# Transposes on TensorE as half transposes side by side, in an attention and mixture kernel

## The chip, the cores and the metric

The kernel runs on one core of one Trainium2 chip. The core has TensorE (PE, with its weight loader PEld), VectorE (DVE), ScalarE (ACT), GpSimd (POOL) and SyncE (SP), which issues most DMAs. Matmuls write PSUM, eight banks of 512 fp32 columns; only PE, DVE and ACT reach it. The metric is the device time of one execution in microseconds, less is better.

## The reference

Inputs are q, k, v of 8 batches, 8 heads, 576 positions and 64 features, and weights of four experts. It computes causal attention in a window of 128 positions with a bias by distance, then a mixture of two out of four experts, each of which is again causal attention over all 576 positions:

```python
scores = where(0 <= rel < 128, q @ k.T / 8 - slope * rel, -1e9)
x = softmax(scores) @ v                      # 8 heads -> 512 features
w = softmax over the two largest of x @ w_gate (0 for the others)
for e in range(4):
    a = softmax(causal((x @ wq[e]) @ (x @ wk[e]).T / 8))
    out += w[e] * (a @ (x @ wv[e])) @ wo[e]
```

## The kernel before

**Windowed attention** goes by head pairs g = 0 to 31, two heads of a batch in one. For each, `attn_s` makes scores in PSUM, DVE adds the bias and takes the row minimum, ACT takes the exponential into a tile w with the row sums, `normalise` scales it (POOL or ACT). `attn_t` turns the nine blocks of 128 by 128 on PE, by a matmul with the identity `idt`, four blocks to a bank: two of them are copied to the tile pa (`evac`, on ACT or DVE), the others are multiplied by a mask in `split`, on DVE alone. `attn_pv` multiplies them by v. The first four pairs go through `half_s`, `half_t` and `half_pv`, in two halves of the positions.

**The mixture** follows batch by batch: `qkproj` and `vproj` (PE, 128 by 128 tiles, the rows `wx,WH`, `wx,WL` and `WH,wx`), `gates`, and for each of two expert pairs pr the scores `moe_s` (tile KKm, 64 by 128 tiles, one expert to each half of the rows) and `moe_s_tail` for the last 64 positions (tile MPL), then `moe_norm`, `moe_t`, `moe_pv`, and `moe_wo` for the output. `moe_t` turns, for a column block c, the blocks of rows i >= c, up to four to a bank, and copies each bank with one `evac`; `moe_t_tail` turns the last rows. The 688 transposes are of 128 by 128 elements.

**The order of everything** is a table. The functions only record operations; some record two alternatives, one for each engine that may do it (`nc.any`, as in `evac`). `plan` reads the table ORDER, which names for each place in the program the operation and its alternative; `_pairs` keeps two matmuls together where the second uses the upper 64 rows. `place` then gives buffers in that order, from pools of equal slots (`_Slots`): all PSUM tiles share eight banks `ps`, SBUF tiles share the pools wx, w5, w10 and w2. Since each recorded operation is emitted at one line, nearly all instructions carry the line L1206; the names of tiles tell them apart. In the names of the profile w is any SBUF slot, ps any bank.

Of the kernel before, what the change touches and what calls it, by code (L numbers as in the profile page):

```python
# [20 lines left out]
DM = H * D  # L21
E = 4
# [20 lines left out]
    "s*f1W`V1-2(vs^s?h-4-=jHwAEiW+H8T*Huw8dV60NC$RQLKSIiPF{ilqD)NJ-R!g};b4CLd*A*7b+;Rpu(-sy+J?NsG~-R>Y7E8&Dqv0t1OV&?!lg-1"
    "rV`PZoS77FwTGzPo(j;84rs@HST_?2HL!Tg+LW3Z<#N!Nf<`l5O%K5Z5?e4NCq&i+S-@&qgN$r|9LR-|ZBO6iOw34HXE4-7PL6fnHWW6e*_{z2slu*A#"
    "5r8bMe9!vHeE`B5(7ah?T>dBn{o;X?Tw{P1w9FaEsiCH#bC(=$g|>yA{wKZ0~{*_kVMR#zk=XE(P~o9+P?&80QnYYQEEtRR&uyItx*p?cH$5kt+4>xm="
    ">pnI9ebEVxzRH!R%K!K=m4|?-f^U%U?>jgaqXkhnZ>%75Bn?<p2DDrKs7VIv;;DKBdm`W#faEvkx>-OQ<`=p$zg#Qdu5DFgvx7x-yfWQye-sIt?rycEn"
    "aH&V=ldtA>J2P}cI&qp~lLj|?Y69A1JL#R#`^b1*uHf*ydu_=J}4mcIDx8+#GPvV|+=LKqvIoSG!}e$_^jauREb1~O)c__Rwfv)orgJD?1x;xW$`t<na"
# [1246 lines left out]
```

## Time and profile before

| | us |
|---|---|
| median of 3 runs (497.78 to 498.13) | 497.96 |
| profiled execution, first to last instruction (its span) | 495.4 |
| PE busy | 487.4 |
| DVE busy | 421.3 |
| ACT busy | 359.3 |
| POOL busy | 222.5 |

The profiled execution is known by its span; the median stands 2.6 us above it. PE's records overlap, as each matmul's duration holds its latency: how long PE needs for one is read from the distance of two starts. A row `ps<-idt,w 128*128 128x128` is a transpose: the loaded tile of 128 rows by 128 columns is w, the moving operand idt has 128 columns. An fp32 matmul that is no transpose stands as two records.

### The profile page before, as it was taken

The numbers are of one execution on the slowest core, as the hardware profiler recorded it, in microseconds if no ns is written. First come the engines' busy times: TensorE is split into PE (matmuls) and PEld (weight loads), VectorE is DVE, ScalarE is ACT, GpSimd is POOL, SyncE is SP. The second block draws the span as 40 slices with busy tenths as digits, with TensorE's granted clock in tenths as the row PEclk, the third lists the DMA queues.
The fourth block names the chain that finished last, engine by engine and source line by source line (L and its number), as shares of the span: only waits on it lengthen the run. The fifth ranks groups of instructions, "written<-read, shape, count | busy, mean of one in ns | idle before, by whom it ended". The sixth has DMA issues, their size and how long they took to land.

```text
span 495.4 us, 16247 instructions
## 1 busy us (share of the span) xinstructions
PE 487.4 (98%) x5772; PEld 430.7 (87%) x5772; DVE 421.3 (85%) x1918; ACT 359.3 (73%) x1349; POOL 222.5 (45%) x440
## 2 busy tenths in 40 slices
PE   7999999999999999999999999999999999999996
PEld 5889988997989889898897988989789897899775
DVE  5999998889997897979989799897999869946763
ACT  4968979878958497585976969587694948543951
POOL 3815575252915246071460815625094533453350
PEclk9999999999999999999999999999999999999999
DMA  7979440027122350234240612623152301200033
GB/s 199 294 183 218 114 116 2 7 45 173 51 74 76 107 140 20 58 94 102 83 131 2 178 32 55 193 81 70 61 150 77 103 2 32 84 1 1 2 107 107
DMA packets 29856, 44.91 MB, mean 91 GB/s; under 512 B 9424, under 2 KB 15824, under 8 KB 29776
## 3 DMA queue, kind: packets, MB, share of 16 engines
q1 hardware_dynamic: 29040, 43.42, 32.7%
q8 instruction: 46, 0.75, 0.6%
q10 hardware_dynamic: 736, 0.46, 0.4%
q14 instruction: 34, 0.28, 0.2%
HBM read 34.42 MB, written 9.44 MB: 89 GB/s over the span
## 4 chain that ended last, share of the span: by engine, by line
PE 69%; DVE 1%; issue 0%; ACT 0%
PE ps L1206 69%; DVE w L1206 1%; DVE ps L1206 0%; ACT AHm L1206 0%; DVE ALTm L1206 0%; DVE nm L1206 0%; DVE ALm L1206 0%; DVE mr L1206 0%
## 5 line engine op out<-in xcount | busy, mean ns | idle before, releaser
L1206 ACT COPY w<-ps 128x512 f32<-128x512 f32 (+3 forms) x165 | 78.7, 504 | 49.3 <-PE ps L1206 42.7
L1206 PE MATMUL ps<-wx,WH 128*128 128x288 f32 (+2 forms) x512 | 110.7, 300 | 0.2 <-DVE nm L1206 0.2
L1206 POOL TENSOR_SCALAR w<-w,mr,w 128x512 f32<-128x512 f32 (+3 forms) x128 | 76.4, 609 | 74.5 <-DVE mr L1206 50.8
L1206 ACT ACTIVATE w<-w,nm 128x128 f32<-128x128 f32 x252 | 98.7, 395 | 7.9 <-DVE nm L1206 7.6
L1206 PEld LDWEIGHTS ps<-wx,WH 128*128 128x128 f32 x512 | 83.0, 189 | 2.5 <-DVE ps L1206 0.3
L1206 ACT ACTIVATE w<-w,mnm 128x128 f32<-128x128 f32 (+3 forms) x128 | 70.9, 556 | 14.5 <-DVE mnm L1206 12.7
L1206 PE MATMUL ps<-idt,w 128*128 128x128 f32 x608 | 80.9, 275 | 0.0
L1206 DVE CUSTOM_DVE_ANT_0 w<-ps,tbt 128x128 f32<-128x128 f32 x288 | 72.8, 284 | 5.2 <-PE ps L1206 4.2
L1206 POOL TENSOR_SCALAR w<-w,r 128x128 f32<-128x128 f32 x151 | 54.7, 373 | 49.0 <-DVE r L1206 37.0
L1206 DVE TENSOR_TENSOR w<-ps,tmt 128x256 f32<-128x256 f32 (+2 forms) x96 | 71.2, 771 | 2.8 <-PE ps L1206 2.4
L1206 PEld LDWEIGHTS ps<-idt,w 128*128 128x128 f32 x608 | 68.9, 140 | 3.9 <-issue 1.1
L1206 PE MATMUL ps<-wx,WL 128*128 128x288 f32 (+2 forms) x256 | 70.8, 296 | 0.0
L1206 PE MATMUL ps<-w 64*64 64x192 f32 (+3 forms) x1256 | 59.8, 306 | 2.1 <-DVE ps L1206 1.3
L1206 PE MATMUL ps<-WH,wx 128*128 128x260 f32 x288 | 61.6, 286 | 0.0
L1206 PE MATMUL ps<-w,vt 64*64 64x192 f32 (+4 forms) x1344 | 57.2, 284 | 0.5 <-DMA vt<-in_vd 0.5
L1206 DVE COPY w<-ps 128x512 f32<-128x512 f32 (+3 forms) x85 | 47.5, 565 | 9.2 <-PE ps L1206 8.6
L1206 PEld LDWEIGHTS ps<-w,vt 64*64 64x64 f32 (+1 forms) x1344 | 48.9, 133 | 6.7 <-issue 1.0
L1206 PEld LDWEIGHTS ps<-w 64*64 64x64 f32 (+1 forms) x1256 | 44.4, 134 | 9.1 <-DMA w<-in_hd 2.3
L1206 ACT ACTIVATE w<-w,r 128x128 f32<-128x128 f32 x137 | 48.4, 396 | 5.1 <-DVE r L1206 4.9
L1206 DVE COPY_PREDICATED ps<-mkt,ps 128x256 f32<-128x256 int32 (+2 forms) x160 | 50.5, 329 | 1.4 <-PE ps L1206 0.4
L1206 DVE CUSTOM_DVE_ANT_0 w<-ps,mtt 128x384 f32<-128x384 f32 (+2 forms) x96 | 50.0, 550 | 0.9 <-PE ps L1206 0.7
L1206 PE MATMUL ps<-w,w 128*64 128x64 f32 (+4 forms) x576 | 48.2, 319 | 0.1
(110 smaller groups left out, 978.2 us busy)
## 6 DMA issues: line engine op xcount, KB each, us to landing
w<-in_hd SPq DMA_DIRECT2D x56, 288.0 KB, 4.5
vt<-in_vd SPq DMA_DIRECT2D x28, 320.0 KB, 4.0
out<-w SPq DMA_DIRECT2D x31, 256.0 KB, 3.8
w<-in_hd SPq DMA_DIRECT2D x14, 128.0 KB, 3.8
w<-in_hd SPq DMA_DIRECT2D x56, 32.0 KB, 3.6
w<-in_wall SPq DMA_DIRECT2D x4, 386.0 KB, 5.4
out<-w SPq DMA_DIRECT2D x8, 128.0 KB, 2.7
vt<-in_vd SPq DMA_DIRECT2D x4, 192.0 KB, 6.3
```

What stands on the lines that cost most here:

```text
L1206: getattr(getattr(tc.nc, e), m)(*a, **k)
```

## The change

608 transposes of 128 rows become 1216 of 64 rows by 128 columns. `turn` takes up to eight blocks and two banks; rows 0 to 63 of each block go to the first bank, rows 64 to 127 to the second, in 64 columns for each block, so a pair of instructions uses the two row halves of PE. Each bank is emptied apart, into every second group of 64 columns of the target. `attn_t` turns eight blocks in one call, with two copies of 128 columns and two masks of 768; `moe_t` has four calls for each expert pair, of 8, 8, 4 and 4 blocks, and the last block whole. The 80 that stay whole are those of `half_t` (32), `half_t_tail` (4), the ninth block of `attn_t` (28) and the last block of `moe_t` (16). `_pairs` now holds the two halves together. The SBUF pool w10 has three slots instead of four, w2 six instead of ten, and pools w4 and w1 are new. The table ORDER is another one throughout.

```diff
--- before.py
+++ after.py
@@ -36,85 +36,81 @@
 
 
 ORDER = (
-    "c-obC0azr*b>?)}>#p9N*3L*X5@XF+j20wDfdm}Jh8Sc>zy}t{@C6dc!6&%D9oQfb7Mwr^8@wRF24ryHyf~~44#;5bN~{Go*bu=9EO0=9c=-%5_#lA`Y"
...
+    "c-p;re_Ui)b!WYIPrZBT_onO3)N`uVst5|PP?!M&89G7)1%+&pfd~m~U_!az!e_vMf&qnT$bf>vPNQ_}j`Ro$hTcFzo9<co1Pmy>(_~=-3LnA14j33|2NG"
...
@@ -194,7 +190,7 @@
     two = {}
     for i in range(1, len(ops)):
         e, m, a, k = ops[i]
-        if e != "tensor" or m != "matmul":
+        if e != "tensor":
             continue
         if any(x.ap[0][1] == D and x.offset // x.ap[0][0] >= D for x in a[:2]):
             assert ops[i - 1][0] == "tensor"
@@ -257,8 +253,10 @@
     ps_s = ps_t = ps_a = _Slots(psum, 8, 512, "ps", PSUM)
     xp = _Slots(cp, 5, 2 * S + TAIL, "wx")
     pp = big5 = _Slots(cp, 8, 2 * S + 3 * D, "w5")
-    tp = big10 = _Slots(cp, 4, 2 * (S + TAIL + S), "w10")
-    big2 = _Slots(cp, 10, DM, "w2")
+    tp = big10 = _Slots(cp, 3, 2 * (S + TAIL + S), "w10")
+    tw = _Slots(cp, 4, 2 * DM, "w4")
+    tr = _Slots(cp, 3, P, "w1")
+    big2 = _Slots(cp, 6, DM, "w2")
 
     busy = {"act": 0.0, "dve": 0.0}
 
@@ -560,38 +558,37 @@
 
     ptT = {}
 
-    def split(dst, src, n):
+    def split(dst, src, n, f=0):
         k = src.shape[1]
-        w = tmt[:, :, :n].unsqueeze(1).broadcast_to((P, k, 2, n))
+        w = tmt[:, :, f : f + n].unsqueeze(1).broadcast_to((P, k, 2, n))
         nc.vector.tensor_tensor(dst, src.unsqueeze(2).broadcast_to((P, k, 2, n)), w, mul)
         busy["dve"] += 65 + 1.04 * 2 * k * n
 
+    def turn(name, blocks):
+        ts = [ps_t.tile([P, 8, D], F32, tag="t", name=f"{name}{x}") for x in "lh"]
+        for k, src in enumerate(blocks):
+            for h in range(2):
+                d = slice(D * h, D * h + D)
+                nc.tensor.transpose(ts[h][:, k, :], src[d], idt[d, d])
+        return ts
+
     def attn_t(g, u):
         pt = state[g][2]
-        t = ps_t.tile([P, 4, P], F32, tag="t", name=f"t{g}_{u}")
         if u == 0:
-            ptT[g] = tp.tile([P, PTW], F32, tag="pa", name=f"pa{g}")
-        w = ptT[g]
-        if u < 2:
-            for k in range(4):
-                nc.tensor.transpose(t[:, k, :], pt[:, 5 * (k % 2) + 2 * u + k // 2, :], idt)
-            i = 2 * u
-            if u == 0:
-                evac(w[:, : 4 * P].rearrange("p (h n) -> p h n", h=2)[:, :, :P], t[:, 0:2, :], 2 * P)
-                split(diag_pair(w, 1, 1, P), t[:, 2:4, :], P)
-            else:
-                
-                for k in range(2) if K["sh"] else (None,):
-                    if k is None:
-                        split(diag_pair(w, 2, 2, P), t, P)
-                    else:
-                        split(diag_pair(w, 2 + k, 1, P), t[:, 2 * k : 2 * k + 2, :], P)
+            w = ptT[g] = tp.tile([P, PTW], F32, tag="pa", name=f"pa{g}")
+            ts = turn(f"t{g}", [pt[:, 5 * (k % 2) + 2 * j + k // 2, :] for j in range(2) for k in range(4)])
+            for h in range(2):
+                c = slice(D * h, D * h + D)
+                evac(w[:, : 4 * P].rearrange("p (h n) -> p h n", h=2)[:, :, c], ts[h][:, 0:2, :], P)
+                split(diag_pair(w, 1, 3, D, D * h), ts[h][:, 2:, :], D, D * h)
         else:
+            w = ptT[g]
+            t = ps_t.tile([P, 4, P], F32, tag="t", name=f"t{g}_{u}")
             nc.tensor.transpose(t[:, 0, :], pt[:, 4, :], idt)
             split(diag_pair(w, NQ, 1, TAIL), t[:, 0, :].rearrange("p (h n) -> p h n", h=2), TAIL)
 
-    def diag_pair(w, i, m, n):
-        a = w[:, 4 * P * (i - 1) + P :]
+    def diag_pair(w, i, m, n, f=0):
+        a = w[:, 4 * P * (i - 1) + P + f :]
         return _View(bass.AP(tensor=a.view.tensor, offset=a.offset, ap=[a.ap[0], [2 * P, 2 * m], [3 * P, 2], [1, n]]), a.tensor)
 
     xT = {}
@@ -837,22 +834,24 @@
             scl2(st["p"][pr, "tail"][:, :S], r[:, 0:1], r[:, 1:2])
         busy["dve"] += 300
 
-    def moe_t(b, pr, c, js):
+    def moe_t(b, pr, u):
         st = m2s[b]
-        t = ps_t.tile([P, 512], F32, tag="t", name=f"mt{b}_{pr}_{js[0]}_{c}")
-        pc = big2.tile([P, 512], F32, tag="pt", name=f"mpt{b}_{pr}_{js[0]}_{c}")
-        n = 512 - P * c
-        for k, j in enumerate(js):
-            for i in range(c, NQ):
-                o = n * k + P * (i - c)
-                nc.tensor.transpose(t[:, o : o + P], st["p"][pr, j, i][:, P * c : P * (c + 1)], idt)
-            st["pt"][pr, j, c] = pc[:, n * k : n * k + n]
-        m = n * len(js)
-        if c == NQ - 1:
-            nc.tensor.transpose(t[:, m : m + P], st["p"][pr, "tail"][:, NQ * P :], idt)
-            st["pt"][pr, "tail"] = pc[:, m : m + P]
-            m += P
-        evac(pc[:, :m], t[:, :m], m)
+        parts = ([(0, 0), (1, 0)], [(0, 1), (0, 3), (1, 1), (1, 3)], [(0, 2), (1, 2)], [("tail", c) for c in range(NQ)])[u]
+        n = 8 if u < 2 else 4
+        pc = (tw if u < 2 else big2).tile([P, n * P], F32, tag="pt", name=f"mpt{b}_{pr}_{u}")
+        blocks = []
+        for j, c in parts:
+            i = [c] if j == "tail" else range(c, NQ)
+            st["pt"][pr, j, c] = pc[:, P * len(blocks) : P * (len(blocks) + len(i))]
+            blocks += [(st["p"][pr, j] if j == "tail" else st["p"][pr, j, k])[:, P * c : P * (c + 1)] for k in i]
+        ts = turn(f"mt{b}_{pr}_{u}", blocks)
+        for h in range(2):
+            evac(pc.rearrange("p (a n) -> p a n", n=P)[:, :, D * h : D * h + D], ts[h][:, :n, :], n * D)
+        if u == 3:
+            t = ps_t.tile([P, P], F32, tag="t", name=f"mt{b}_{pr}_4")
+            nc.tensor.transpose(t, st["p"][pr, "tail"][:, NQ * P :], idt)
+            pc = st["pt"][pr, "tail", NQ] = tr.tile([P, P], F32, tag="pt", name=f"mpt{b}_{pr}_4")
+            evac(pc, t, P)
 
     def moe_pv(b, pr, c):
         st = m2s[b]
@@ -875,25 +874,15 @@
             act_copy(AH[:, pr, :512], acc, 512)
             dve_sub(AL[:, pr, :512], acc, AH[:, pr, :512].bitcast(F32), 512)
 
-    def moe_t_tail(b, pr):
-        st = m2s[b]
-        pt = st["p"][pr, "tail"]
-        pcl = big2.tile([P, 512], F32, tag="pt", name=f"mptl{b}_{pr}")
-        t = ps_t.tile([P, 512], F32, tag="t", name=f"mtl{b}_{pr}")
-        for c in range(NQ):
-            nc.tensor.transpose(t[:, P * c : P * c + P], pt[:, P * c : P * c + P], idt)
-        evac(pcl, t, 512)
-        st["ptl"] = pcl
-
     def moe_pv_tail(b, pr):
         st = m2s[b]
-        pcl, pcl2 = st["ptl"], st["pt"][pr, "tail"]
+        pt = st["pt"]
         V2 = st["v2"]
         acc = ps_t.tile([P, 512], F32, tag="t", name=f"mal{b}_{pr}")
         for c in range(NQ + 1):
             for j in range(2):
                 e = 2 * pr + j
-                src = pcl[:, P * c + D * j : P * c + D * j + D] if c < NQ else pcl2[:, D * j : D * j + D]
+                src = pt[pr, "tail", c][:, D * j : D * j + D]
                 nc.tensor.matmul(
                     acc[D * j : D * j + D, :TAIL], V2[:, c, D * e : D * e + D], src,
                     start=(c == 0), stop=(c == NQ),
@@ -1015,11 +1004,11 @@
             else:
                 for c in range(NQ):
                     moe_pv(b, pr, c)
-            live[0] -= 2 if tail else 5
+            live[0] -= 0 if tail else 7
         pend.append((f, 0, b))
 
     def room(n):
-        while live[0] + n > K["tp"]:
+        while live[0] + n > K["tp"] and pend:
             flush()
         live[0] += n
 
@@ -1038,9 +1027,9 @@
             return u
 
         def t_units(g):
-            tt = [(w, lambda c=c: attn_t(g, c)) for c, w in enumerate((0.44, 0.44, 0.12))]
+            tt = [(w, lambda c=c: attn_t(g, c)) for c, w in enumerate((0.88, 0.12))]
             pv = [(2.1, lambda: run(g))]
-            orders = ("tttp",)
+            orders = ("ttp",)
             return tag(g, [(tt if ch == "t" else pv).pop(0) for ch in orders[K["apv"]]])
 
         marks = []
@@ -1084,12 +1073,8 @@
         return us
 
     def t_units(b, pr):
-        us = []
-        for c in range(NQ):
-            for js in ((0,), (1,)) if c < 2 else ((0, 1),):
-                us.append((0.11 * (4 - c) * len(js), lambda c=c, js=js: (room(1), moe_t(b, pr, c, js))))
+        us = [(0.7, lambda u=u: (room((2, 2, 1, 2)[u]), moe_t(b, pr, u))) for u in range(4)]
         us.append((K["pw"], lambda: part(b, pr, 0)))
-        us.append((0.55, lambda: (room(1), moe_t_tail(b, pr))))
         us.append((K["pw"], lambda: part(b, pr, 1)))
         return us
 
```

On PE, behind a group of projections in the middle of the program, before: the transposes (`idt`) follow one at a time, each into the bank of its block (MPL is the tail's tile).

```order
L1206 MATMUL ps_69<-wx_81,WL 128x288
L1206 MATMUL ps_69<-wx_77,WH 128x288 x2
L1206 MATMUL ps_74<-wx_77,WL 128x288
L1206 MATMUL ps_69<-wx_77,WL 128x288
L1206 MATMUL ps_72<-idt,w_86 128x128
L1206 MATMUL ps_71<-idt,MPL_119 128x128 x2
L1206 MATMUL ps_73<-idt,w_89 128x128
L1206 MATMUL ps_76<-idt,w_85 128x128
```

The same engine and kind of place now: two rows to each block, in two banks, one behind the other.

```order
L1191 MATMUL ps_70<-wx_80,WL 128x288
L1191 MATMUL ps_70<-wx_77,WH 128x288 x2
L1191 MATMUL ps_70<-wx_77,WL 128x288
L1191 MATMUL ps_72<-wx_77,WL 128x288
L1191 MATMUL ps_71<-idt,w_84 128x64
L1191 MATMUL ps_74<-idt,w_84 128x64
L1191 MATMUL ps_75<-idt,MPL_121 128x64
L1191 MATMUL ps_76<-idt,MPL_121 128x64
L1191 MATMUL ps_75<-idt,MPL_121 128x64
L1191 MATMUL ps_76<-idt,MPL_121 128x64
```

Transposes stood in the tile shape of the projections; now they stand in pairs of halves, and the shape changes behind the fourth row, where none changed before.

On DVE, at the attention's masks of one pass (`tmt` is the mask; the row of 448 columns is other work), before: masks of 256, 512 and 1024 columns for the tile w_91, of 1024 and 256 for the next.

```order
L1206 TENSOR_TENSOR w_91<-ps_73,tmt 128x2x2x64
L1206 TENSOR_TENSOR w_91<-ps_74,tmt 128x2x2x128
L1206 TENSOR_TENSOR w_91<-ps_75,tmt 128x4x2x128
L1206 TENSOR_TENSOR w_92<-ps_73,tmt 128x4x2x128
L1206 TENSOR_TENSOR w_96<-w_96,ps_71 128x448
L1206 TENSOR_TENSOR w_92<-ps_69,tmt 128x2x2x64
```

The same stretch now: two masks of 768 columns (6x2x64), one copy of 128 and the mask of 256.

```order
L1191 TENSOR_TENSOR w_90<-ps_75,tmt 128x6x2x64
L1191 COPY w_90<-ps_75 128x2x64
L1191 TENSOR_TENSOR w_90<-ps_69,tmt 128x6x2x64
L1191 TENSOR_TENSOR w_90<-ps_73,tmt 128x2x2x64
L1191 TENSOR_TENSOR w_92<-ps_74,tmt 128x2x2x64
```

The mask over four blocks and that over two have become two over six half blocks, and a copy of the first two half blocks stands between them.

On ACT, copies out of PSUM in the middle of the program, behind the projections' results, before: a bank to a copy, of 384 or 512 columns.

```order
L1206 CAST KKm<-ps_75 128x288
L1206 CAST QHm<-ps_76 128x288
L1206 CAST KKm<-ps_74 128x288
L1206 COPY w_97<-ps_72 128x384
L1206 COPY w_102<-ps_70 128x512
L1206 COPY w_101<-ps_75 128x384
L1206 COPY w_100<-ps_73 128x512
```

The same place now: copies of 8x64, 4x64 and 2x64 columns, one for each half.

```order
L1191 CAST QHm<-ps_70 128x288
L1191 CAST KKm<-ps_72 128x288
L1191 CAST KKm<-ps_69 128x288
L1191 COPY w_102<-ps_76 128x512
L1191 COPY w_100<-ps_74 128x4x64
L1191 COPY w_93<-ps_71 128x8x64
L1191 COPY w_91<-ps_72 128x2x64
L1191 COPY w_94<-ps_69 128x8x64
L1191 CAST QJm<-QLm 64x64
L1191 COPY w_94<-ps_76 128x8x64
```

The copies of 384 columns are gone; those of half blocks go to the same slot two by two (w_94).

## Rows read from the trace of the kernel before

**Rows 1.** Page, part 1: engine, busy us (share of the span) xinstructions

```profile
PE 487.4 (98%) x5772; PEld 430.7 (87%) x5772; DVE 421.3 (85%) x1918; ACT 359.3 (73%) x1349; POOL 222.5 (45%) x440
```

**Rows 2.** Chain of waits in order of time: start us, us, what

```profile
175.89 148.14 PE ps L1206 x1661
...
329.07 162.59 PE ps L1206 x1665
```

**Rows 3.** What PE waited for: us in total, times, longest us; first, last

```profile
PE ps L1206 <- DVE ps L1204: 1.3, 1, 1.3
...
PE ps L1206 <- DVE nm L1206: 0.2, 1, 0.2
```

**Rows 4.** Windows: us, busy of each engine, PEclk, DMA share, GB/s

```profile
25.00:50.00 25.00, 25.00 (x373) 22.02 (x371) 24.22 (x127) 19.50 (x87) 9.53 (x24) 1.00 0.85 199
50.00:75.00 25.00, 25.00 (x353) 23.28 (x350) 24.78 (x121) 21.98 (x92) 16.00 (x33) 1.00 0.43 113
125.00:150.00 25.00, 24.92 (x342) 21.83 (x341) 23.72 (x103) 18.52 (x70) 12.90 (x19) 1.00 0.28 77
225.00:250.00 25.00, 25.00 (x359) 21.53 (x360) 24.05 (x108) 19.05 (x71) 5.89 (x11) 1.00 0.38 92
425.00:450.00 25.00, 25.00 (x282) 23.12 (x281) 16.28 (x59) 11.26 (x38) 10.72 (x17) 1.00 0.01 1
```

**Rows 5.** Windows, the transposes alone (tile idt): PE, PEld

```profile
125.00:150.00 25.00, 5.48 (x43) 4.76 (x43) 1.00 0.28 77
225.00:250.00 25.00, 4.32 (x37) 3.75 (x34) 1.00 0.38 92
```

**Rows 6.** Timeline, PE, 26 transposes: start us, us, what

```profile
284.69 3.00 PE L1206 MATMUL ps<-idt,w 128*128 128x128 f32 x26
```

**Rows 7.** Timeline, PE, transposes, then KKm pairs

```profile
167.60 0.71 PE L1206 MATMUL ps<-idt,w 128*128 128x128 f32 x5
168.24 0.39 PE L1206 MATMUL ps<-KKm,QHm 64*128 64x256 f32 x2
168.46 0.28 PE L1206 MATMUL ps<-KKm,QLm 64*128 64x256 f32 x2
168.58 0.28 PE L1206 MATMUL ps<-KKm,QHm 64*128 64x256 f32 x2
```

**Rows 8.** Groups by form, PE: shapes xcount | busy us, mean ns

```profile
L1206 PE MATMUL ps<-w,vt 64*64 64x192 f32 x672 | 35.2, 327 | 0.5 <-DMA vt<-in_vd 0.5
...
L1206 PE MATMUL ps<-w,vt 64*64 64x64 f32 x448 | 19.3, 220 | 0.0
```

**Rows 9.** Timeline, PE, transposes behind 64 by 64 tiles

```profile
251.17 0.66 PE L1206 MATMUL ps<-idt,w 128*128 128x128 f32 x4
```

**Rows 10.** What the weight loader waited for; longest total first

```profile
PEld ps L1206 <- issue: 21.6, 98, 0.4
```

**Rows 11.** Groups by form, ACT

```profile
L1206 ACT COPY w<-ps 128x384 f32<-128x384 f32 x33 | 15.5, 484 | 3.3 <-PE ps L1206 1.5 <-DVE w L1206 1.5
...
L1206 ACT COPY w<-ps 128x256 f32<-128x256 f32 x42 | 15.4, 369 | 26.4 <-PE ps L1206 23.2 <-DVE w L1206 2.1 <-DVE lg L1206 0.8
...
L1206 ACT COPY xq<-ps 128x64 f32<-128x64 f32 x13 | 2.7, 205 | 3.6 <-PE ps L1206 3.6
```

**Rows 12.** Groups by form, DVE

```profile
L1206 DVE TENSOR_TENSOR w<-ps,tmt 128x1024 f32<-128x1024 f32 x32 | 38.8, 1218 | 1.3 <-PE ps L1206 1.1
...
L1206 DVE TENSOR_TENSOR w<-ps,tmt 128x512 f32<-128x512 f32 x32 | 21.5, 679 | 0.5 <-PE ps L1206 0.5
```

**Rows 13.** Window of 46 transposes (tile idt): PE, PEld, PEclk

```profile
472.80:478.00 5.20, 5.12 (x46) 4.97 (x46) 1.00 0.77 252
```

More of the change, by code (lines that the diff above doesn't have):

```diff
@@ L43 @@
[L43 to L47, printed above, removed]
@@ new lines @@
+    "~0fe35wx$nLDK~K*|lRx(LQ1$BlxcA(1zUO<s=Z;0NJpGjA;$xP;@m?n*EKb&xLSV#6loDtm3HihhZu@970F1K?5(mXs>8MLfWA=Qz+a5PLHt$esp+O<`="
+    "l+W}NAp=uhBtx?kXd3^G}pk*q<ku`78k$|zX})rtJCJHqeWkRI)O$eR+1*FW<$izEpRHdo-k0U!bUHWj}<GldQ|%T4Y(T}bBT}y<rJEr@gzRmuI&2OPU2f"
+    "4VQo2<4bM}B9xpCUZZEB_*#@V2=50!S-PGN*+=$u+M~!#<b~`M>!WKk91qIK$-b*XOE?#Kw7HLeB?cGnTtlL}0B5sc-W#H19z2na2p5*16<_wb2oB`>H*L"
+    "%hQvS8uTjT(Bp7258MwqAmM`C4vk%I(%w=&ObV!WPLG*yHVX)y}jOnPq@?ek$f*_b5{dcjntGKtJZ_>fsVBFW|ozfczXwVw?paUKu8gk?4u(e)BOVGZq7h"
@@ new lines @@
+    "I4LL$SS5a?cnH-Z@7V#==t!Gpi_S?&uw{E_0mwinX(B)p9j|SuZNT@(>L3RoAp-_)c6JZlx+WKUbHf$)PV|Cv5;|AbWAbU{lrIMufULT~o9~SaQ{NdC9_8"
+    "|}l+_rULf7tsd31Jn0(3w-bhWo8F3;5f*ff_yZ)FoNYnPJ}*+Ft8xC=cIw+~o()+c_iw)Nm+U%Cn!M7n!l`0wjZ>UHlV)A%#AF9jeK06!re7q)}n%I`i4s"
+    "|)K%DREH?(l>;c@4Wrv6)H|3+mxsdn+D(jCtopM8r?l;Z5q^iYZ40yWmnxW46%`Y<^4T<gUT)rRaH_3)sS+_1ykd4OeDA!hzD<xLNcn=ikecz#R}^{0dU7"
+    "agzXG4qPg5j*{85;hv_BhRhTF)P-xaoZ?0FrgGU<w7@NFPK2E*4so8L(<jJZm6Q-bhW&j@i(I;t*^Pe)`1>gmGm*(W^uT3L>x#5jTplo}_Rvk%APLK3mHi"
@@ new lines @@
+    "1s4u7mcj_I0R8&pMt=o2g$62dKT3y|2RA@mYVSLY3CF!gNxc7*}v*&t42U`G_s%dF;3LD9}IraQ=qVuFzPSR<K%{m>glb)({oG+eGiM?UR*RGUs7+FMi=N"
+    "`4mh{>!vJ>+nr8u;IAo607)!(;lGUx!A0`5ff1sE?E!co8axrM@hewf`D>VnI@&)1I6fN~8M=8YQ*yGiO_nw_dfnEzw^MU@<LNOrGBG=obh68A(UG#|Ncx"
+    "aCM(O|q4%fJU(?^)*t8a>1ych3QJtsSETiNTM2irzzg>RKl*oe*nH!wS;H}Pi<@fD=neW1EjsBMDET&=lk6dla=H=zh1DlKWXBK>xHY}{zST}jQu5IZ9id"
+    "W%a(atbaL<bLmqfAZ&%3z5M7=4nvLgXh1&{r;bFokbswGSIt(bK2%Mape~zLU-ryA%0<$-vCUNp*j4h+W73JD+c((Y=zB_Q26v~5IB&n;AbLe90|Ss&<Fg"
@@ new lines @@
+    "_IHVWhSKig$RjL2*#uK6?<*5|YpRqa{$Qmw_%Ff8B<~BIvk4#)i7OVv@Pa-_S9o^GgswC>y;YqPQ+pZ?t6vd?|u}rnAa;_(>)HhbbhR#Z}b7EI$k<;$12M"
+    "b2aatJUBFpxl^>GZwr2YV|K_xK<@n8)j5aZ>zC<!#Z26pz&z(gw}LBaO{nl}e#n9j<iK!37<kZP1xt)YPk{5kk~C#a?M+v(Ws1|A7>$$u6d3MJv?P2Z{Zj"
+    "Ihc<QPu$+f>17VtX+POrtgLHPp}L{b&g6*9?|g)@-(>H=Op61!>P>Hd>0QU@wCnpvJGs(V&{Wui-8F7s(jbHrqSy)3vVHTo5IjD2p>XVDF>iAgzvp67WEN"
+    "FE@b`EzMuYhKB{R}x!YY6KWg6icUjF9S>=SdU;dR$vz0oMKFV5#lpKrDKl({w<pUucvcvo@*G9TrSw07WEtE>?!tF)#lpD-Iw=Z0E-v!XQqgVtgxUF?mfk"
@@ new lines @@
+    "tuSr+fGtqAeK2&Zcv^LKmaVqEH)z2$I(2%4vr2_y)GzA<`7_&h;&;&DA~>>UImBm66WZhgiJyzY-F;GM#BE`Jvy(rGu4SZ$LzL3M<$pXrcbjovwLq`g(_R"
+    "Al2W3^v&iV(n=ia`9hq)6H6yieXVD$bNawsCcSXLf`>^wA;ZNW9YZAOt^aj7i{kRNQ%b@~FX5l(CZl<b>(A*|JagmfJuK7NF;aU_~pW}~igJlapwhHqQr="
+    "m)J@ajyNmAtfkYFU8ge&090@$#S1#3ObLjDs6wLR>$2#|VGZ;RXnYSR{o5%q5K9%=83Zf^OyZAr7d}_ld**^wS%E@ju`8b__I@(<2+OQ$`-haDWjyeBfzl"
+    "Qf2hq8N7b{eYK~)8fZUv<iz~MtbJkK#uUdCxwCmZ;b6|GiUB$mPoMf~1W@-ve6zmt)i^{G;>GYoRJgJ32#{?Rl}fRGkpe67NuPO9ls;J(uFzJzgrs(JKt0"
@@ L118 @@
+    "%0vbuMoZDkGQzV4Bh<}@dGtOI(3%@NGb;9~k@qa{1Y@*NDG&C*b8%jF<^(|Qd6PJ7`AcUm6L7-sp2MMU!P@Xj!M*fU+uF?c+ktMiIL5Lvy;$2ut;&tRr4D"
+    "|o|_<zIj`(X"
 )
```

125 lines of the change are left out of this document (52 added, 73 removed).

## Prediction

> **What bounds the kernel now.** I read the page's busy lines first, then the chain of waits, PE's own waits, windows of busy time, and last single stretches of the timeline and the groups by form. PE is busy in 98% of the span, DVE in 85%, ACT in 73% [rows 1]. The chain that ended last runs through PE for 148.14 us and again for 162.59 us with nothing between its matmuls [rows 2]. PE waits for another engine only five times, 1.3 us at most [rows 3]. So PE's stream is the bound: what is taken out of it is gained as far as DVE, ACT and POOL keep up. DVE is the next in line, and in places as full as PE: 49.0 of the 50 us from 25 to 75, 23.7 and 24.1 of 25 in two later windows [rows 4].
>
> A busy share does not give the price of a matmul, since matmuls overlap; the step from one start to the next does. Twenty-six full transposes in a row take 3.00 us, of which the last one's own duration is 0.27: (3.00 - 0.27) / 25 = 0.109 us each [rows 6]. The 608 transposes that change hold 608 x 0.109 = 66.3 us of PE's 495.4.
>
> **The half transposes.** Each of the 608 becomes two instructions, for rows 0 to 63 and rows 64 to 127, that write 64 columns each into two banks. The trace has no such instruction, so I bound the price of a pair from both sides.
>
> Side by side: the KKm scores are pairs of 64 rows by 128 columns already. Two such matmuls of 256 columns show a union of 0.28 us, as long as one of them, and the pairs start 0.12 us apart (168.46, 168.58) [rows 7]. So two row halves run together, their weight loads included.
>
> The moving side: a 64-column fp32 pass lasts 220 ns and a 192-column one 327 [rows 8], hence 107 / 128 = 0.84 ns a column, 54 ns for 64 columns.
>
> The weight side could spoil it, for each half still loads 128 columns. Where a run of transposes starts behind another tile shape, the first load is not hidden. Four transposes then take 0.66 us, and 0.66 - 0.27 - 2 x 0.109 = 0.17 is the first step [rows 9]. It exceeds 0.109 by 0.06, so the load of 128 columns takes about 0.06 us. For the KKm pairs the same excess is (168.46 - 168.24) - 0.12 = 0.10 us [rows 7]: the load of a transpose is the cheaper kind.
>
> A pair therefore takes 0.054 to 0.06 us, or, if the load held it, up to the 0.109 of a full transpose. I take 0.057, nearest to both the moving side and the exposed load. 608 x (0.109 - 0.057) = 31.6 us leave PE.
>
> The Trainium skill speaks against this: TensorE: Matmul & The Clock Gate, section "LDWEIGHTS (loading the stationary operand)", puts a load at columns / 1.2 ns whatever the rows, an estimate of 107 ns for a half as for a whole. By it a pair would be held there and nothing would be saved. The KKm load agrees with it, 0.10 us; the transpose load, 0.06 us, does not, and the trace decides.
>
> **Changes of tile shape.** Before, a transpose had the 128 by 128 shape of the projections and stood among them free of charge. Now it has not. Counted over the two built programs, PE changes its tile shape 116 times before and 157 times after. A change costs a drain and a first load. The drain: the last of five transposes starts at 167.60 + 0.71 - 0.27 = 168.04, the KKm pair behind it at 168.24, 0.20 later instead of 0.109, so 0.09 [rows 7]. The load is 0.06 or 0.10 as above. Together 0.15 to 0.19; the gaps that the profile gives the weight loader with no releaser, 21.6 us over 98, are 0.22 each [rows 10], the upper end. At 0.17, 41 x 0.17 = 7.0 us come back (6 to 9). Nothing hides this, PE being the bound.
>
> **Evacuations.** A turn of eight blocks fills two banks, each emptied apart. For each of the 16 MoE head pairs, copies of 4 x 512 and 3 x 384 columns become 4 x 512, 4 x 256 and 1 x 128. On ACT 384 columns cost 484 ns, 256 cost 369 and 64 cost 205 [rows 11], so 128 about 0.26: 3 x 0.48 = 1.45 becomes 4 x 0.37 + 0.26 = 1.74 us, 4.6 us over the 16. In attention a copy of 256 columns becomes two of 128: 28 x (2 x 0.26 - 0.37) = 4.2 us. The products with the mask, of 1024 and 512 columns (1.22 + 0.68 us), become two of 768, which lies midway at 0.95: the same 1.90 [rows 12]. The steps of 64 columns in what is written I put at nothing: one per cent of the copies would be 1 us, on engines that wait for PE. These 9 us lie on ACT and DVE, beside PE. The order also moves work between engines: 25 scalings from ACT to POOL, 11 differences from POOL to DVE, and three of the four subtractions that make WL (772 columns) too. Summed by groups DVE gets some 3 us more (424) and ACT some 4 (363). ACT's idle time of 136 us covers that; DVE has 74.
>
> Where DVE has no cover I charge it. In the first 75 us PE wins little, since the 36 transposes of half_t and half_t_tail stay whole, while the WL subtractions add 3 x 0.95 us (772 columns lie midway between the 512 and 1024 of [rows 12]) where DVE is full: 2 us, as some of it finds a gap. In the window from 125, with 43 transposes [rows 5], PE would need 25 - 43 x 0.052 + 0.35 (its share of the shape changes) = 23.1 against DVE's 23.7; in that from 225, with 37, 23.4 against 24.1: 1.2 us more. The longest runs of half transposes, 64 to 96 of them, ask for 8 to 12 banks; a turn takes PE 8 x 0.057 = 0.46 us, and the copies of its two banks 0.6 to 0.7 us on ACT and DVE: some 0.2 us a turn beyond the eighth bank, under 1 us in all, left to the range.
>
> **The sum.** 495.4 - 31.6 + 7.0 + 2 + 1.2 = 474.0 us of span. The median of the runs, 497.96, stands 2.6 above the span of the profiled execution, so 476.6, and I say 476. What is late next is DVE: 424 busy of 474, 89%.
>
> **Rivals.**
> VectorE keeps its idle time. DVE idles 74 us now, and not for want of work: its waits for PE, ACT and POOL are links of one chain of score, minimum, exponential, scaling and transpose. The forecast leaves it 474 - 424 = 50. If only half of that 24 us goes, the time is 424 + 62 + 2.6 = 489. For it: DVE over 95% in several windows. Against it: PE's five short waits show that the order has kept PE supplied so far, and from 425 DVE has room, 16.3 of 25 [rows 4].
> The Trainium skill, TensorEngine Tiling (Array Packing), "PSUM Bottleneck", states that tiling speeds PE up but not the emptying of PSUM; the copies above agree and put its size at 9 us over two engines.
>
> The load holds the pair. If a half's load is of the KKm kind, 0.10 us, or two halves take turns at the loader, 2 x 0.06, a pair takes about 0.109, PE saves nothing and pays 7 us for shapes: 497.96 + 7 = 505, slower. The point from which it decides is a pair of 0.109 - 7.0 / 608 = 0.097 us. For it: a load of 0.10 is in the trace. Against it: that is another operation's, and 0.06 is this one's.
>
> The clock falls. If PE were granted 1.2 instead of 2.4 GHz in runs of half transposes, these pairs would take 0.114 us: 476 + 34.7 = 511. Against it: in a window with 46 full transposes the granted clock was 1.00 [rows 13].
> The Trainium skill, TensorE: Matmul & The Clock Gate, "Part 4: PE-mode transpose", says that transposes don't count as activity for the full clock; this row does not agree.
>
> Another loss of the new order (a landing, a buffer, three big slots instead of four) isn't worked out; it would show as PE waits of several us on DMA or POOL.
>
> **How the numbers follow.** Forecast 0.73, DVE 0.15, load 0.08, clock 0.01, another loss 0.03. The forecast's own range is 469 to 484: the pair at 0.054 to 0.06 (2 us either way), shapes -1 to +2, DVE's charge from nothing to 8 instead of 3.2. The range for 8 in 10 reaches into the DVE rival: 467 to 492. Between 497.0 and 499.0 a measurement can't tell this kernel from no change. Faster: 0.73 and 0.14 of the DVE case, 0.87; slower: 0.08 + 0.01 + 0.02 = 0.11; the 0.02 left lie within.
>
> **What would show it.** Sixteen half transposes in a row take about 8 x 0.057 + 0.2 us, the two of a pair start within 0.01 us of each other; near 0.11 a pair, the load rival is right. PE's waits on DVE of over 10 us in total would show the DVE rival; in the forecast DVE is busy about 424 us, 89%. A granted clock under 0.99 in mid-span would show the clock. A time over 492 or under 467 makes the prediction wrong, and pairs at 0.08 make its first step wrong even where the time fits.

## The result: 0.7% slower, 501.5 us

The kernel after takes 501.49 us (500.92 to 501.96, 4 runs), the kernel before on the same chip 497.87 (497.39 to 498.13, 4 runs). The ratio is 1.0067, 95% interval [1.0053, 1.0081]: slower, where 476 us were forecast. The granted clock was 0.998, and the profiled span is 499.4 us, 4.0 more than before's.

From the page of after: the busy line, and the shares of the chain that ended last, by engine.

```profile
PE 482.0 (97%) x6380; PEld 411.5 (82%) x6380; DVE 428.3 (86%) x1936; ACT 365.1 (73%) x1375; POOL 221.1 (44%) x456
...
PE 45%; DVE 35%; POOL 6%; ACT 5%; issue 4%; DMA 3%; SPq 1%; ACTq 0%; DVEq 0%; POOLq 0%
```

Against [rows 1], PE has shed only 5 us of busy time (busy counts from issue to end, waits inside included), and DVE is at 428.3 us, up 7.0 where the forecast counted 3 (424). DVE's idle time, 499.4 - 428.3 = 71.1 us, is nearly that of before (74). And the chain has another shape: in before it ran through PE for 148 and 163 us at a stretch [rows 2]; here 35% of it lies on DVE. (The profile follows the chain of before back to 145 us, that of after to the start.)

The half transposes themselves did what the forecast says. The timeline shows 34 halves in a row, and the group by form all 1088 of the tile w (start, length, or busy us and mean ns, then the idle time before them):

```profile
322.16 1.24 PE L1191 MATMUL ps<-idt,w 64*128 64x64 f32 x34
```

```profile
L1191 PE MATMUL ps<-idt,w 64*128 64x64 f32 x1088 | 47.1, 227 | 2.6 <-POOL w L1191 1.0 <-DVE KKm L1191 0.6 <-DVE mnm L1191 0.4
```

Thirty-four halves are 17 pairs: (1.24 - 0.23) / 16 = 0.063 us a pair, where [rows 6] gave 0.109 for a whole transpose. That is also the median over the whole trace; of the pairs that follow a pair, a tenth take 0.11 or more. Each pair loads 2 x 128 columns of weights in that time. The Trainium skill, TensorE: Matmul & The Clock Gate, "LDWEIGHTS (loading the stationary operand)", would have each of these loads take an estimated 107 ns; the trace does not agree.

What went wrong shows in the waits of PE and of its weight loader (us in total, times, longest). The first fence is the matmuls', the second the loader's, the third the loader's in before.

```profile
PE ps L1191 <- DVE nm L1191: 3.2, 9, 0.9
PE ps L1191 <- POOL w L1191: 2.3, 6, 0.6
...
PE ps L1191 <- DVE lg L1191: 0.8, 1, 0.8
PE ps L1191 <- ACT w L1191: 0.7, 1, 0.7
```

```profile
PEld ps L1191 <- issue: 22.9, 97, 0.5
PEld ps L1191 <- DVE nm L1191: 8.6, 20, 1.1
PEld ps L1191 <- POOL w L1191: 6.2, 16, 0.8
PEld ps L1191 <- DVE w L1191: 4.9, 20, 0.4
PEld ps L1191 <- ACT w L1191: 4.5, 13, 1.2
```

```profile
PEld ps L1206 <- ACT w L1206: 2.9, 12, 0.4
...
PEld ps L1206 <- DVE w L1206: 2.1, 9, 0.3
PEld ps L1206 <- DVE nm L1206: 1.5, 5, 0.4
...
PEld ps L1206 <- POOL w L1206: 0.5, 2, 0.3
```

Before, PE waited 4.0 us in five places [rows 3]; now 11.1 us in 27. With the loader's rows that name another engine (19.3 us before, 37.8 after, added over all rows of the view; a wait of the loader that goes on as one of the matmul may stand in both) that is 23.3 us before and 48.9 after: 25.6 us of new waiting, nearly what the forecast lacks (501.5 - 476 = 25.5). That the two are so near is partly chance: below, a table with 28 us less of this waiting gains 22. The row "issue", in which the forecast saw the upper end of the price of tile-shape changes, hardly moved from the 21.6 us of [rows 10].

The windows that answer to [rows 4] (busy us and instructions of each engine, then the granted clock):

```profile
50.00:75.00 25.00, 24.71 (x382) 22.24 (x381) 24.64 (x113) 20.31 (x84) 17.73 (x39) 1.00 0.31 82
125.00:150.00 25.00, 23.89 (x364) 20.37 (x362) 23.83 (x111) 20.23 (x74) 12.92 (x24) 1.00 0.31 97
225.00:250.00 25.00, 24.70 (x348) 20.34 (x347) 24.07 (x113) 19.00 (x70) 11.48 (x28) 1.00 0.23 63
425.00:450.00 25.00, 24.26 (x321) 21.55 (x321) 19.21 (x67) 16.23 (x53) 11.20 (x21) 1.00 0.12 44
```

PE was full in them before; now it lacks 0.3 to 1.1 us in each, at full clock, while DVE stands at 23.8 to 24.6 of 25 in the first three. DVE was as full there in before (24.8, 23.7, 24.1), with PE full beside it; so its share alone doesn't tell why PE now waits. One stretch of the chain shows how this looks (start, length, what; for every piece the chain names what the end waited for):

```profile
122.06 0.20 DVE w L1191
122.28 0.20 DVE w L1191
122.49 0.20 DVE w L1191
122.70 0.20 DVE w L1191
...
127.48 0.16 DVE w L1191
127.74 0.17 DVE w L1191
127.98 3.71 PE ps L1191 x29
131.85 0.41 issue
132.26 0.41 ACT w L1191 x2
...
137.97 0.53 DVE w L1191
138.70 0.20 DVE w L1191
...
139.77 5.23 PE ps L1191 x61
```

From 119.8 to 128.0, and again, after a stretch of ACT, from 134.5 to 139.8, the chain is, but for issues of at most 0.18 us, one DVE instruction behind another. PE works meanwhile, on matmuls that the chain does not name; what decides, as I read it, is how soon DVE's queue comes to the products that PE's later work reads.

### The profile page after: what moved, and what is told of

Read it like the earlier page. It is cut to its first block, busy times and chain, and to the rows that moved or that the text cites. A ratio compares the mean times of both kernels' runs of the same rounds, so it can differ in the third digit from the quotient of the medians.

```text
span 499.4 us, 17525 instructions
## 1 busy us (share of the span) xinstructions
PE 482.0 (97%) x6380; PEld 411.5 (82%) x6380; DVE 428.3 (86%) x1936; ACT 365.1 (73%) x1375; POOL 221.1 (44%) x456
## 4 chain that ended last, share of the span: by engine, by line
PE 45%; DVE 35%; POOL 6%; ACT 5%; issue 4%; DMA 3%; SPq 1%; ACTq 0%; DVEq 0%; POOLq 0%
PE ps L1191 45%; DVE w L1191 21%; DVE ps L1191 6%; POOL w L1191 5%; ACT w L1191 4%; DMA w<-in_hd 2%; DVE mr L1191 1%; SPq L1191 1%; DVE ALm L1191 1%; DMA w<-in_wall 1%; DVE r L1191 1%; DVE wx L1191 1%; DVE KKm L1191 1%; DVE MPL L1191 1%; DVE nm L1191 0%
## 5 line engine op out<-in xcount | busy, mean ns | idle before, releaser
L1191 ACT COPY w<-ps 128x256 f32<-128x256 f32 (+2 forms) x217 | 87.7, 441 | 36.7 <-PE ps L1191 25.8
L1191 POOL TENSOR_SCALAR w<-w,r 128x128 f32<-128x128 f32 x176 | 66.1, 387 | 100.5 <-DVE mr L1191 29.7
L1191 POOL TENSOR_SCALAR w<-w,mr,w 128x512 f32<-128x512 f32 (+3 forms) x128 | 80.0, 634 | 45.0 <-DVE ps L1191 13.5
L1191 ACT ACTIVATE w<-w,mnm 128x512 f32<-128x512 f32 (+3 forms) x128 | 71.1, 557 | 17.2 <-DVE mnm L1191 16.5
L1191 DVE TENSOR_TENSOR w<-ps,tmt 128x768 f32<-128x768 f32 (+3 forms) x96 | 72.3, 772 | 1.8 <-PE ps L1191 1.2
L1191 PE MATMUL ps<-idt,w 64*128 64x64 f32 (+1 forms) x1152 | 62.1, 231 | 6.3 <-POOL w L1191 2.3
L1191 PEld LDWEIGHTS ps<-idt,w 64*128 64x128 f32 (+1 forms) x1152 | 48.9, 139 | 18.3 <-POOL w L1191 6.0
L1191 DVE CUSTOM_DVE_ANT_0 w<-ps,mtt 128x256 f32<-128x256 f32 (+2 forms) x96 | 50.2, 553 | 1.2 <-PE ps L1191 0.4
L1191 PEld LDWEIGHTS ps<-WH,wx 128*128 128x128 f32 x288 | 48.0, 189 | 2.0 <-DVE nm L1191 0.3
L1191 DVE COPY w<-ps 128x256 f32<-128x256 f32 (+3 forms) x93 | 42.5, 477 | 7.9 <-PE ps L1191 7.6
## 6 DMA issues: line engine op xcount, KB each, us to landing
w<-in_hd SPq DMA_DIRECT2D x14, 128.0 KB, 3.9
out<-w SPq DMA_DIRECT2D x8, 128.0 KB, 2.4
```

Source lines behind the costliest of these rows:

```text
L1191: getattr(getattr(tc.nc, e), m)(*a, **k)
```

## The experiments

Two theories stood at first. **O**: TensorE's stream still sets the time, and after's sequence fails to feed it. **V**: VectorE, with waits that no sequence removes, is as long as TensorE, so that a shorter stream gains nothing. All times are medians of device microseconds; ratios are to the kernel before on the same chip.

### Whole transposes in the order of after

```diff
 def turn(name, blocks):
...
-            for h in range(2):
-                d = slice(D * h, D * h + D)
-                nc.tensor.transpose(ts[h][:, k, :], src[d], idt[d, d])
+            t = ts[k % 2].rearrange("p a n -> p (a n)")[:, P * (k // 2) : P * (k // 2) + P]
+            nc.tensor.transpose(t, src, idt)
```
(and the same number of evacuations and mask products, each now on whole blocks)

> The kernel after with its order of the instructions, its buffers and its list of evacuations kept, but each pair of half transposes replaced by one whole 128x128 transpose (blocks alternate between the two banks). Theory O (the order): TensorE's stream still sets the time, and the new order only makes it wait about 25 us more; then the pair step of 0.062 us goes back to 0.109 us (608 x 0.047 = +29 us), some 40 tile-shape changes at 0.17 us go (-7 us), and the time is about 523 us (515 to 530). Theory V (VectorE): VectorE's work with its idle time is now as long as TensorE's, in any order; its instructions do not change here, TensorE merely fills its waits, and the time stays at 500 to 509 us.

518.73 us, ratio 1.0423 [1.0389, 1.0457]: in O's range, outside V's. With whole transposes, after's table, buffers and copies together cost 518.7 - 498.0 = 20.7 us, and the halves give 518.7 - 501.5 = 17.2 back. The chain still lies for over two fifths on other engines:

```profile
PE 56%; DVE 27%; POOL 4%; DMA 4%; ACT 4%; issue 3%; SPq 1%; ACTq 0%; DVEq 0%; POOLq 0%
```

TensorE's length counts, but in this order for 17.2 us of the 24.6 that the forecast gave to pairs and shapes.

### A shorter TensorE stream in both orders

```diff
-        nc.tensor.transpose(t[:, k, :], src, idt)
+        nc.tensor.matmul(t[:, k, :], src_hi_bf16, idt_hi_bf16, start=True, stop=True)
```
(once in the whole-transpose form of after, once in before; the views take the upper 16 bits of each number)

> As the run with whole transposes in the order of after, but each is one bfloat16 matmul of the upper 16 bits of its block against the identity (about 0.055 us, 128x128 tiles; the transposed values are rounded). It leaves out the low half of the numbers. It gives after's order a TensorE stream that is shorter than after's own: no shape changes at the pairs (-7 us) and 608 x 0.007 = -4 us. Theory O: 501.5 - 8 to 11 = 490 to 494 us, and against the whole transposes 33 us less. Theory V: 497 to 502 us, and against the whole transposes at most 10 us less.

497.89 us, ratio 0.9998 [0.9984, 1.0013]: 3.6 us under after and 20.8 under whole transposes in the same order; between O and V. The gain that was counted, 33 us, is some 31: a bfloat16 block takes (1.09 - 0.22) / 15 = 0.058 us (0.22 is the last one's own duration), and 608 x (0.109 - 0.058) = 31.

```profile
111.30 1.09 PE L1194 MATMUL ps<-idt,w 128*128 128x128 bf16 x16
```

> The kernel before with its own order, buffers and evacuations, its 608 transposes replaced by the same bfloat16 matmuls of 0.055 us (low half of the numbers left out). TensorE's stream is shorter by 608 x 0.054 = 33 us, and nothing else moves. Theory O: before's order hands TensorE its work in time, so most of it is gained: 468 to 478 us. Theory V: VectorE has 74 us of idle time that waits on chains through other engines and does not shrink with TensorE; the time falls by at most half, 482 to 496 us.

489.81 us, ratio 0.9838 [0.9805, 0.9871]. It lies in V's range and is a miss for O as I had put it: with nothing moved, before's own order passes on 8.2 of 31 us. Its weight loader now waits more for DVE and ACT (2.1 and 2.9 us in before):

```profile
PEld ps L1210 <- DVE w L1210: 6.1, 22, 0.6
PEld ps L1210 <- ACT w L1210: 4.8, 16, 0.8
```

In all, PE and its loader wait 40.2 us for other engines here, 23.3 in before. The few waits of [rows 3] had told that before's sequence fits before's durations, not that DVE and ACT had room for a faster PE.

### Less VectorE work in after

```diff
-                split(diag_pair(w, 1, 3, D, D * h), ts[h][:, 2:, :], D, D * h)
+                split(diag_pair(w, 1, 3, D // 2, D * h), ts[h][:, 2:, : D // 2], D // 2, D * h)
```

> The kernel after with its 56 VectorE mask products of 768 elements cut to 384 (the other half of each is left out), about 56 x 0.4 = 22 us less VectorE work, TensorE and order unchanged. Theory O: VectorE is not the limit, the time stays within 5 us, 496 to 501 us. Theory V: VectorE's work is what the end follows, and 15 to 22 us go: 480 to 487 us.

497.95 us, ratio 0.9997 [0.9984, 1.001]: 19.6 us of DVE busy time went (428.3 to 408.7), and 3.5 us of the time. V, by which DVE's work is what the end follows, fails here. O's range (496 to 501) holds, though 3.5 us clear of the noise went, which a DVE that never holds PE would not give. What was left was that particular DVE instructions hold PE, by their place in the queue.

### Other tables of order

The table of order was then searched anew, with a list of five in-order queues and the durations, hand-over times and shape prices of the traces; the instructions and the pools of buffers stay as they are; which slot of a pool a tile gets follows from the order and changes with it.

```diff
 ORDER = (
-    "c-p;re_Ui)b!WYIPrZBT_onO3)N`uVst5|PP?!M&89G7)1%+&pfd~m~U_!az!e_vMf&qnT$bf>vPNQ_}j`Ro$hTcFzo9<co1Pmy>(_~=-3LnA14j33|2NG"
...
```

> The kernel after with nothing changed but its table of order: the same instructions, buffers and half transposes, put into another sequence on each engine (and some evacuations and products moved between VectorE, ScalarE and GpSimd). The sequence was searched for with the durations, hand-over times and tile-shape prices of the two traces; played through with these, the queues of after end at 494 us (499 measured) and the new ones at 474 us. Theory O (the table of after does not fit its new durations; TensorE can be kept supplied): 476 to 484 us. Theory V (VectorE, with waits that no order removes, is as long as TensorE): 492 us or more.

495.66 us, ratio 0.9948 [0.9933, 0.9963]: in V's range, and a miss for O by 12 us. Its trace shows a wait that the search had not known (ACT's copies out of a transpose bank; in brackets the idle time before, and for whom):

```profile
55.65 1.72 ACT L1190 COPY w<-ps 128x128 f32<-128x128 f32 x5 [0.62 <-DVE w L1190]
86.86 1.25 ACT L1190 COPY w<-ps 128x128 f32<-128x128 f32 x3 [0.78 <-DVE w L1190]
```

The DVE instruction that they wait for is the mask product that reads the same bank. In the built programs a bank's users wait for each other in their order, readers too; halves put two evacuations and two products onto each pair of banks.

> The control: the kernel before, its table of order searched in the same way from its own table. The search finds 1 us. Both theories: 494 to 499 us, no difference that tells them apart; a gain of over 5 us would mean that the new sequences gain by something other than the fit to the half transposes.

509.18 us, ratio 1.0218 [1.0193, 1.0244]. The control became slower, outside its range. Of the 11 us, 2.2 are one wait for a DMA and about 3.4 the clock behind it (an estimate, 20 x 0.17 in one window, last section); the rest was not traced singly, but the second control, made with the rule below, comes to 501.

> The re-planned table of after with whole 128x128 transposes in place of the pairs of halves. Theory O: TensorE's stream sets the time in this order, so the 608 pair steps count in full: 0.047 x 608 = 29 us more, less about 40 tile-shape changes at 0.11 to 0.17 us = 4 to 7 us, so 22 to 25 us above the run with halves, 499 to 508 us. Theory V: at most 10 us above it.

513.46 us, ratio 1.0308 [1.029, 1.0326]: 17.8 us above the run with halves, between the two theories.

> The kernel before with bfloat16 transposes of 0.057 us (the low half of the numbers left out), its table searched anew for these durations. Theory O: the 25 us that before's own table did not pass on (489.8 measured, 33 us of TensorE work gone) come with a table that fits: played through with the trace's durations it ends at 463 us, so 464 to 472 us. Theory V: 482 us or more.

486.75 us, ratio 0.9769 [0.9749, 0.9789]: in V's range and a miss for O, 3 us under before's own table; the search lacked that rule here too.

With the rule that a bank's users follow one another, the tables were searched again:

> Again the kernel after with nothing changed but its table of order. The first re-planned table (495.7 us) lost to waits that its plan did not hold: in its trace ScalarE's copy out of a transpose bank waits for VectorE's mask product that reads the same bank (up to 0.9 us each), and the other way round. This table is searched with that rule (two engines do not work on one PSUM bank at a time) and ends at 474 us with the traces' durations, where after's own table ends at 496 us (499 measured). Theory O (the table does not fit): 475 to 483 us. Theory V (VectorE with its waits is as long in any order): 492 us or more.

**479.51 us, ratio 0.9631 [0.9601, 0.966]**: in O's range, 18 us below before and 22 below after with after's instructions (some on another engine) and pools. From its page, the busy line and the chain by engine; then the chain in the stretch that was shown for after:

```profile
PE 469.4 (98%) x6380; PEld 409.8 (86%) x6380; DVE 416.5 (87%) x1891; ACT 367.4 (77%) x1388; POOL 236.0 (50%) x488
...
PE 90%; DMA 3%; SPq 2%; POOL 2%; DVE 1%; ACT 0%; issue 0%; DVEq 0%; ACTq 0%
```

```profile
118.87 18.07 PE ps L1188 x235
136.94 0.04 issue
136.98 3.05 PE ps L1188 x53
```

The chain lies on PE again, 235 pieces without a break. PE and its loader wait 20.6 us for others (before 23.3, after 48.9), and DVE idles 476.8 - 416.5 = 60.3 us.

> The control: the table of the kernel before, searched in the same way and with the same rule, whole transposes as before. The search finds 2 us in it. Both theories: 493 to 499 us. The first control came out at 509 us, 5 us of it in the start, where TensorE's granted clock fell to 0.8 in three slices; if that comes again, up to 505 us.

501.24 us, ratio 1.0074 [1.0051, 1.0098]: 2 us above the range of 493 to 499, without the fall of the clock that was to excuse more (granted 0.996). The search finds nothing in before, so the 22 us are not a gift of the search.

> The table of the second re-planned run with whole 128x128 transposes in place of the halves: what the halves are worth in an order that keeps TensorE supplied. Theory O: they count in full, 608 x 0.047 = 29 us less 4 to 7 us of tile-shape changes, so 22 to 25 us above the run with halves (498 to 507 us). Theory V: under 10 us above it.

505.06 us, ratio 1.0144 [1.0114, 1.0174]. In a table that feeds PE, halves are worth 505.1 - 479.5 = 25.5 us, just above O's 22 to 25. That O's number fits is luck in part: it took off 4 to 7 us for tile-shape changes, but counted in the traces PE changes its tile shape 147 times with halves in this table and 152 times with whole transposes. So 25.5 is the pairs alone, where 608 x (0.109 - 0.063) = 28.0 would be due.

With whole transposes this table is 7.5 us slower than before on the same chip, though PE and its loader wait no longer (19.2 us against 23.3). PE changes its tile shape 36 times more than in before (116); at the forecast's 0.17 that would be 6 us, an estimate that no run tests. Against before, the halves in their table thus give 25.5 - 7.5 = 18 us.

### What in the table costs

First the sequence alone: the edit is again another table, in which every instruction stays on the engine on which after has it.

> The kernel after with its table of order changed in the sequence alone: every instruction stays on the engine that after's own table gives it (in the re-planned run 350 evacuations, scalings and subtractions had moved, and VectorE had 18 us less work). Theory S (the sequence costs): the durations of the traces end this table at 476 us, 2 us above the re-planned one, so 478 to 486 us. Theory E (the engine choice costs, VectorE has too much work): 490 us or more.

483.00 us, ratio 0.9696 [0.9677, 0.9716]: theory S. The sequence, with the slots that follow from it, gives 18.5 of the 22 us. It is not by fewer changes of tile shape: PE makes 160 here, 157 in after. With DVE's work left as it was:

```profile
PE 473.3 (98%) x6380; PEld 410.0 (85%) x6380; DVE 426.2 (88%) x1936; ACT 364.2 (76%) x1375; POOL 219.6 (46%) x456
```

DVE is busy 426.2 us, as in after, but idles 482.2 - 426.2 = 56.0 instead of 71.1.

Then one cut in three tables:

```diff
-            nc.vector.copy_predicated(s[:, 2 * P : 3 * P], mkt[:, :P], s[:, P : 2 * P])
+            nc.vector.copy_predicated(s[:, 2 * P : 2 * P + D], mkt[:, :D], s[:, P : P + D])
...
-        tc.nc.vector.memset(t[D:, : 3 * P].rearrange("p (a n) -> p a n", n=P)[:, :, :D], 0.0)
+        tc.nc.vector.memset(t, 0.0)
```
(the form for two bands likewise)

The last two lines are a second change, against the "nothing else changed" of the expectation: at the start DVE clears eight whole banks, before PE's first scores. The first row is of after, the second of after with the cut:

```profile
L1189 DVE MEMSET ps<- 64x192 f32 x8 | 1.7, 218 | 0.8 <-PEq L1264 0.8
L1189 DVE MEMSET ps<- 128x512 f32 x8 | 3.9, 485 | 1.3 <-PEq L1264 0.9
```

In all three runs PE's eleventh matmul comes 2.44 us later by it, and of the 12.9 us of DVE busy time 9.2, 7.4 and 8.0 are left as net savings (after, before, searched table).

> The kernel after with 128 of VectorE's predicated copies (the wrapped bands of the attention scores) cut to half their columns (the other half is left out): 64 x 0.134 + 64 x 0.067 = 12.9 us less VectorE work, nothing else changed. Theory D (in after's sequence TensorE hangs on VectorE's queue): most of it is gained, 8 to 11 us, 490 to 494 us. Theory P (the loss lies in TensorE's own sequence, its tile-shape changes and banks): under 3 us, 498 to 502 us.

494.63 us, ratio 0.9932 [0.9917, 0.9947]: 6.9 us gained in after, between the two ranges and nearer to D's.

> The same cut of 12.9 us of VectorE work in the kernel before. TensorE's stream is the bound there: both theories 1 to 4 us, 494 to 497 us. A gain as large as in after would mean that VectorE holds TensorE in before as well, and theory D tells nothing of the table.

498.28 us, ratio 1.0009 [0.9995, 1.0022]: no gain, where 1 to 4 us were expected.

> The same cut in the re-planned kernel of 479.5 us. If its table has freed TensorE from VectorE's queue (theory D), the cut is worth nothing: 477 to 480 us. If VectorE is near the bound in it too, 469 to 474 us.

479.76 us, ratio 0.9639 [0.9619, 0.9659]: no gain against 479.51, as D has it.

The chains by engine, of the cut in after and of the cut in before:

```profile
PE 59%; DVE 28%; ACT 5%; POOL 4%; issue 3%; ACTq 0%; DVEq 0%; POOLq 0%
```

```profile
PE 97%; DMA 1%; DVE 1%; SPq 0%; POOL 0%; ACT 0%; issue 0%
```

The same cut gives 6.9 us in after's table and nothing in the other two. Counted from the eleventh matmul, behind the longer clearing, PE gains 9.3 us in after, 2.6 in before and 1.4 in the searched table, so "nothing" may hide 1 to 3 us; the contrast stays. In after's sequence these copies stand in the chain, 100 of the 160 with 26.4 us; in before's, as far as it is followed, 7 do, and in the searched one none: there they lie beside PE. But a place in the chain is no price. The mask products are 24.8 us of after's chain, and cutting their work by 19.6 us gave only 3.5.

### Before with short transposes and a table made for them

> The kernel before with its 608 transposes as bfloat16 matmuls of 0.057 us (the low half of the numbers left out), and its table searched anew for these durations, with the rule that two engines do not work on one PSUM bank at a time (the first such table, without the rule, gave 486.8 us; before's own table 489.8). Played through with the traces' durations it ends at 463 us, and the tables made in this way so far came out 3 to 6 us above their plan. Theory O (a sequence fits only the durations it was made for): 466 to 474 us. Theory L (the layout holds them): 482 us or more.

485.38 us, ratio 0.9765 [0.974, 0.979]: a miss for O, in L's range. PE is hardly held by others, though. In this run PE and its loader wait 24.1 us for others instead of 40.2, and the chain by engine is

```profile
PE 91%; DMA 3%; DVE 2%; ACT 1%; issue 1%; SPq 0%; POOL 0%; DVEq 0%
```

so PE is fed, yet the profiled span is 19 us longer than the 463 of the plan. Which of PE's steps are longer, I have not settled. The run gives O no support: in before a table made for the shorter transposes brings 4.4 us, not the 23 that its own table had not passed on.

In one view (us; the bfloat16 runs in a line of their own):

| table of order | whole transposes | halves |
|---|---|---|
| before's | 497.9 | |
| after's | 518.7 | 501.5 |
| searched, with the bank rule | 505.1 | 479.5 |

Bfloat16: 489.8 in before's own table, 485.4 in its searched one, 497.9 in after's.

## Why the prediction was wrong

- **The pairs.** 0.063 us instead of 0.057; 608 x 0.006 = 3.6 us too much gain was counted.
- **Pairs and shapes together.** 31.6 - 7.0 = 24.6 us were forecast. The 25.5 between the two kernels of the searched table look like a match and are none: there the changes of tile shape are 147 and 152, not 157 and 116, so the 25.5 hold no shape term. The pairs alone came to 25.5 of 31.6. The 7.0 for shapes was not isolated by any run.
- **Evacuations.** DVE was to be busy 424 us and is 428.3, ACT 363 and 365.1. The sizes are 2 to 4 us off; neither decides.
- **The step that failed** is the charge for the new order: "Where DVE has no cover I charge it", 2 + 1.2 us, with up to 8 in the range. It rested on PE's five short waits, from which I took that the order keeps PE supplied and that what leaves PE's stream is gained. They were a property of before's table with before's durations: shortened by 31 us with nothing moved, before itself passed on 8.2. And after's is another table. With halves it takes 501.5 against the 479.5 of one that fits, 22 us where 3.2 were charged; with whole transposes the same exchange of tables is worth 518.7 - 505.1 = 13.7. With a table that fits, the forecast's 476 is missed by 3.5 us.
- **The rival "VectorE keeps its idle time"** has the right place. Its price for half of the idle time was 489; the idle time stayed nearly whole, 71.1 of 74. Its sign, over 10 us of PE's waits on DVE, came only with the loader's waits added: PE's matmuls waited 7.6 us on DVE, the loader 22.3. Its reason, that these waits are links of a chain, falls as a limit of the work itself: the run with the sequence alone changed has the same DVE work and 56.0 us of idle time. What keeps DVE idle and then late is the sequence.
- **"Another loss of the new order"**, put at 0.03 and not worked out, is what it was. I had looked for it as waits on DMA or POOL. Waits on DMA did not grow (2.4 us, 3.5 in before); those on POOL for w did, 8.5 us of PE and its loader where 0.5 stood before, and those on DVE (nm, w above all) more, 29.9 where 14.9 stood.
- The rivals of the load and of the clock did not come: pairs of 0.063, granted clock 0.998.

Shown are: that the table, not the halves, makes after slower; that its sequence (with the slots that follow from it) accounts for most; and that in it VectorE's work holds PE, where the same cut frees time in after and hardly any in the other tables. Not shown is which displacements in the table do it, on which engine's queue or by which slots; they were not undone singly. Nor is it shown that any kernel can be given a table that fits: with before's bfloat16 transposes the search found none.

## What to carry to other kernels

A new order is a term of its own: price the old work in the new order before adding what the change saves. That the bound engine hardly waits says that the present sequence fits the present durations; take some per cent from its stream, and the next engine's queue decides, unless a sequence that fits the new durations is found, as it was for the halves. And in such a sequence count as waits not the data alone, but every shared bank: the table searched without that rule took 495.7 us, the one with it 479.5, though the two differ in more than this.

## What I had not expected of the hardware

In the first control one late landing was paid twice. PE's timeline (in brackets the idle time before, and for whom), then windows of that kernel, busy us of each engine and the granted clock:

```profile
55.18 1.42 PE L1201 MATMUL ps<-w 64*64 64x192 f32 x32
58.82 1.46 PE L1201 MATMUL ps<-w,vt 64*64 64x192 f32 x32 [2.22 <-DMA vt<-in_vd]
```

```profile
56.00:60.00 4.00, 1.78 (x53) 1.46 (x49) 2.18 (x12) 2.68 (x11) 3.03 (x7) 0.98 0.82 210
60.00:64.00 4.00, 4.00 (x46) 3.44 (x40) 2.79 (x18) 3.04 (x13) 1.42 (x5) 0.50 0.32 94
64.00:68.00 4.00, 4.00 (x22) 3.90 (x21) 1.87 (x9) 1.66 (x11) 0.62 (x1) 0.66 0.01 2
...
60.00:80.00 20.00, 19.97 (x247) 17.62 (x240) 16.01 (x70) 14.79 (x56) 8.62 (x20) 0.83 0.21 60
```

PE idles 2.2 us for a DMA; then it is full again, but from 60 to 64 at a granted clock of 0.50, the lower of its two levels (1.2 of 2.4 GHz), and over 60 to 80 at 0.83 in the mean. In before no window of [rows 4] is under 1.00, nor in after any of those shown.
